# Banded attention with a top-1 expert layer on one core: the zero fill in two halves, the second round's up weights ahead of the row store

## The chip, the core and the metric

The program runs on one NeuronCore of a Trainium2 chip: a tensor engine (PE) with its own weight loads (PEld), VectorE (DVE), ScalarE (ACT), GpSimd (POOL), SyncE (SP), and 16 DMA engines that the queues of SP, ACT and POOL share. The metric is device microseconds for one execution.

## The reference

Two stages. The first is attention over 2 batches, 8 heads, 768 positions and 64 channels, in which each query sees the keys less than 16 positions away and one summary key and value for every block of 32 positions. The second is an expert layer over the 1536 tokens that result:

```python
logits = x @ w_gate
expert_idx = np.argmax(logits, axis=1)
...
for i in range(N):
    e = expert_idx[i]
    if counts[e] < capacity:
        disp[e, counts[e]] = x[i]
        ...
h = np.maximum(np.einsum('ecd,edf->ecf', disp, w1), 0.0)
y = np.einsum('ecf,efd->ecd', h, w2)
out = np.zeros((N, D), dtype=np.float32)
for i in range(N):
    if keep[i]:
        out[i] = gate_w[i] * y[expert_idx[i], pos[i]]
```

There are 8 experts of 512 x 1024 and 1024 x 512 weights and a capacity of 384 tokens. A row of `out` that no expert writes stays zero.

## The kernel before, in words

**Order.** Every operation has a short name, and the list `SEQ` (line 112) names them one after the other. An engine runs its own instructions in the order in which that list issues them. The framework adds the semaphore waits that the data need, and for DRAM tensors these go by the range of rows that an access names.

**Attention (to about 75 us).** For each batch and pair of heads the scores, their maximum, the exponentials, the turned probabilities and the product with the values run in groups of four blocks of 64 queries. The result of a batch lies in SBUF as `X[b]`: six tiles of 128 tokens, 512 channels, the token's number and its gate weight.

**Routing (`Route`), once per batch.** PE turns `X[b]` and multiplies it by the gate matrix; DVE finds each token's expert and its place there. At its end (`ga0`, `ga1`, line 439) SP stores the batch's rows into the DRAM tensor `xrow`.

**Expert rounds (`Round`).** A round serves one expert with up to 384 tokens. The first (names without a letter) takes an expert's tokens of batch 0 while batch 1 is still being routed; the second (B) and the third (C) take tokens of both batches. Seven more rounds stand in branches that this data does not enter. In a round:

- `lw` and `lW`: SP loads four quarters of the up weights `w1` and four of the down weights `w2`, 512 KB each, into the buffers `w1r` (tag `ld`) and `w2r`.
- `h` and `s`: ACT rounds each quarter to a high part, DVE takes the low rest (lines 580 and 586).
- `fr`: POOL gathers 128 rows of `xrow` by the numbers in `ids` into `xgb` (line 571), three times.
- `T`, `H`, `I`: PE turns the rows (line 599), ACT and DVE split them.
- `u`, `r`, `e`: the up product in eight pieces (line 625), the ReLU on ACT (630), the rest on DVE (634).
- `D`: the down product in three pieces of 128 tokens (line 642); `y`: ACT scales it by the gate weight (652).
- `P`: POOL writes the 128 rows of `y` to `out` by their token numbers (line 655); padded places have numbers beyond the bound and are dropped.

**The zero fill.** `zr` sets one tile `zrow` to zero on POOL, and `fill` lets SP write it over all of `out` (line 731). A put must come behind the fill of the rows that its access names, since the put's rows have to survive.

**What else sets the order.** The second round's gather reads all of `xrow` and so needs the stores of both batches. The first round's gather names batch 0 alone. The choice of the third round's expert reaches SP by a register load of `r0ei` (line 661), ahead of which SP stands until DVE has written it.

Of the kernel before, what the change touches and what calls it, by code (L numbers as in the profile page):

```python
# [10 lines left out]
F32 = mybir.dt.float32  # L11
# [26 lines left out]
NTOK = N // P  # L38
TPB = S // P
# [5 lines left out]
EARLY = TPB  # L45
# [65 lines left out]

SEQ = """
q1 k1 t0 S0 k2 z2 t2 S1 M0 q2 Q11a M1 Q10p E0 w1p q3 kb1 E1 S2 kp1p vb0 R0 z3 R1 M2 t1 K0 S3 K1 k3 kb2 E2 v0 w2p vt0 M3 v2 vk0 vb2 S4 kp2p E3 vP0 v1
R2 Q21a M4 S5 q4 Q20p K2 t3 E4 Q30p k4 R3 M5 Q31a vp0 S6 vb1 E5 zr misc t4 R4 M6 w3p q6 S7 K3 kb3 v3 E6 vt1 M7 V00 kp3p q5 vk1 K4 V01 vp1 N00 N00 vP1
R5 N01 N01 E7 S8 K5 R6 M8 S9 K6 E8 R7 M9 vt2 vk2 V10 E9 vP2 V11 N10 N10 Q41a Q40p S10 N11 N11 K7 vp2 k5 vb3 R8 S11 M10 t5 K8 w4p kb4 E10 R9 M11 vt3
kp4p V20 vk3 K9 vP3 V21 N20 E11 vb4 S12 vp3 N21 t6 N20 Q60p k6 Q61a N21 R10 M12 k7 R11 K10 S13 E12 vt4 K11 M13 V30 vk4 V31 E13 Q50p N30 N30 S14 N31
Q51a N31 w5p kb5 R12 x0 M14 K12 kp5p x1 vb5 X0a x2 X1a S15 t7 vb6 X2a q7 E14 v6 vt5 M15 l00 w6p vk5 kb6 v5 R13 L00a E15 R14 w7p v4 kb7 x3 g00 K13 v7
S16 X3a kp6p vb7 K14 vP4 x4 M16 x5 Q70p X4a S17 X5a vp4 Q71a vt6 kp7p E16 M17 l01 vp5 R15 vP5 L01a E17 S18 vk6 g01 K15 M18 vp6 R16 ch0 S19 vP6 E18 ch0
ch0 ch0 ch0 R17 ch0 ch0 M19 S20 ch0 ga0 E19 ga0 ga0 pf0 ga0 pick vt7 M20 V40 vk7 pick pl0 K16 pl0 vP7 pick V41 N40 pl0 K17 N40 S21 N41 pick vp7 N41
pick pl0 pl0 pl0 R18 pick pl0 pl0 E20 R19 V50 pl0 pl0 pl0 pl0 K18 pick M21 V51 K19 N50 pick N50 E21 tk0 S22 N51 pick pick pick pick first N51 lw0 ts0  # L120
pads rows lw1 pads R20 rows pads M22 rows fr0 lw2 S23 K20 lw3 pads E22 pads pads pads firstB R21 fr1 M23 K21 V60 E23 V61 fr2 N60 N60 h10a R22 N61 N61
R23 K22 s10v V70 K23 h11a V71 lW0 lW1 lW2 lW3 fill N70 N70 T0 N71 s11v x6 H0 x7 N71 X6a I0 X7a h12a o0 x8 X8a l10 s12v h13a o1 s13v T1 L10a T2 H1 o2
x9 H2 I1 g10 X9a I2 h20a x10 u0 X10a s20v h21a h22a s21v x11 r0 s22v u1 X11a h23a e0 s23v l11 r1 e1 u2 L11a g11 r2 u3 ch1 e2 ch1 ch1 ch1 ch1 ch1 ch1
u4 r3 ch1 e3 ga1 ga1 ga1 ga1 pf1 r4 cl1 lwB0 u5 pl1 pl1 pl1 lwB1 pl1 e4 pl1 pl1 pl1 pl1 u6 r5 pl1 pl1 pl1 pl1 padsB e5 padsB padsB padsB padsB padsB
padsB tk1 r6 u7 ts1 rd e6 rd rowsB rd rowsB frB0 lwB2 rd rd rd rd rd r7 rd rd rd e7 D0 rd rd frB1 rd rd hB10a rd rd rd rd rd rd rd rd rd set firstC
frB2 lwB3 lWB0 lWB1 lWB2 sB10v lWB3 hB11a nr lwC0 sB11v y0 frC0 lwC1 TB0 hB12a D1 HB0 sB12v P0 lwC2 IB0 hB13a sB13v lwC3 TB1 y1 frC1 TB2 HB1 D2 HB2
IB1 IB2 P1 hB20a sB20v hB21a lWC0 sB21v hB22a lWC1 sB22v uB0 hB23a lWC2 sB23v TC0 rB0 lWC3 uB1 y2 eB0 oB0 frC2 uB2 rB1 P2 hC10a eB1 sC10v rB2 uB3 eB2
oB1 TC1 rB3 uB4 hC11a eB3 sC11v uB5 rB4 eB4 rB5 uB6 hC12a eB5 sC12v uB7 rB6 oB2 eB6 rB7 HC0 eB7 DB0 HC1 IC0 hC13a IC1 sC13v TC2 yB0 PB0 DB1 HC2 IC2
oC0 DB2 yB1 PB1 hC20a sC20v hC21a sC21v hC22a oC1 sC22v uC0 hC23a yB2 PB2 sC23v uC1 rC0 eC0 rC1 uC2 eC1 oC2 uC3 rC2 eC2 rC3 uC4 eC3 uC5 rC4 eC4 rC5
uC6 eC5 uC7 rC6 eC6 rC7 eC7 DC0 DC1 yC0 PC0 DC2 yC1 PC1 yC2 PC2  # L130
""".split()


# [1 line left out]
def attention_moe(ctx: ExitStack, tc: tile.TileContext, qT, kT, vT, vw, wg, w1, w2, cf, cm, cr, cv, out, cap: int):  # L135
    nc = tc.nc
# [5 lines left out]
    big = ctx.enter_context(tc.tile_pool(name="big", bufs=4))  # L142
    work = ctx.enter_context(tc.tile_pool(name="work", bufs=2))
# [22 lines left out]
    r7 = cft[:, C_R7 : C_R7 + E]  # L166
# [24 lines left out]
    kc, qc, vc, vt, kt = {}, {}, {}, {}, {}  # L191
# [313 lines left out]
    bufs = {}  # L505
# [13 lines left out]
    class Round:  # L519
# [131 lines left out]
            self.y[j] = work.tile([P, DM], F32, tag="y", name="y", bufs=2)  # L651
            nc.scalar.activation(self.y[j], self.yp[j], AF.Copy, scale=self.xg[:, j, DM + 1 : DM + 2])  # L652

        def put(self, j):
            nc.gpsimd.indirect_dma_start(  # L655
                out=out, out_offset=bass.IndirectOffsetOnAxis(ap=self.oid[j], axis=0),
                in_=self.y[j], in_offset=None, bounds_check=N - 1, oob_is_err=False,
            )

    def fetch(t, hi, engines=(SP,)):  # L660
# [38 lines left out]
    sel, plans, ops = {}, [], {}  # L699
# [3 lines left out]
    def op(name, f, *a):  # L703
        ops[name] = lambda: f(*a)

    def op_on(name, f, *a):
        for e, eng in ENGINES.items():
            op(name + e, f, *a, eng)

    def chain(name, make):  # L710
        going = []

        def run():
            if not going:
# [9 lines left out]
        nc.scalar.dma_start(out=crt, in_=cr)  # L724

    def zeros():
        sel["zrow"] = work.tile([P, DM], F32, tag="y", name="zrow", bufs=2)
        nc.gpsimd.memset(sel["zrow"], 0.0)

    def fill():  # L730
        nc.sync.dma_start(out=out.rearrange("(t p) d -> p t d", p=P), in_=sel["zrow"].unsqueeze(1).to_broadcast([P, NTOK, DM]))

    def pick():
        key = const.tile([P, E], F32, name="key0")
# [97 lines left out]
    def last_clip():  # L832
        sel["cl"] = clip(RB.cn, "b")

    for c in range(2 * HP):
        op(f"k{c}", load_k, c)
        op(f"q{c}", load_q, c)
        op(f"t{c}", load_vt, c)
        op(f"v{c}", load_v, c)
        op_on(f"w{c}", windows, c)  # L840
        for h in range(2):
            op_on(f"Q{c}{h}", queries, c, h)
            op(f"V{c}{h}", values, c, h)
# [13 lines left out]
    for r, rt in enumerate(routes):  # L857
# [8 lines left out]
        op(f"pf{r}", rt.prefix)  # L866
        chain(f"pl{r}", rt.place)
        chain(f"ga{r}", rt.gate)
    for name, f in dict(misc=misc, zr=zeros, fill=fill, nr=count, set=settle, tk0=census, tk1=last_census, ts0=first_tokens, ts1=all_tokens, cl1=last_clip).items():
        op(name, f)  # L870
    for name, f in dict(pick=pick, rd=lambda: rounds(0)).items():
        chain(name, f)
# [1 line left out]
    def on_round(i, name, f, *a):  # L874
        op(name, lambda: getattr(R[i], f)(*a))

    for i, c in enumerate(["", "B", "C"]):
        op(f"first{c}", begin, i)
        if i < 2:
            chain(f"rows{c}", lambda i=i: rows(i))  # L880
            chain(f"pads{c}", lambda i=i: pads(i))
        for g in range(4):
            on_round(i, f"lw{c}{g}", "load_w1", (g,))
            on_round(i, f"lW{c}{g}", "load_w2", (g,))
            for e, eng in ENGINES.items():
                on_round(i, f"h{c}1{g}{e}", "high_w1", g, eng)
                on_round(i, f"s{c}1{g}{e}", "low_w1", g, eng)
                on_round(i, f"h{c}2{g}{e}", "high_w2", g, eng)
                on_round(i, f"s{c}2{g}{e}", "low_w2", g, eng)
        for j in range(RT):  # L890
            op(f"fr{c}{j}", rows_fetch, i, j)
            on_round(i, f"T{c}{j}", "turn", j)
            on_round(i, f"H{c}{j}", "turn_high", j)
            on_round(i, f"I{c}{j}", "turn_low", j)
            on_round(i, f"D{c}{j}", "down", j)
            on_round(i, f"o{c}{j}", "place", j)
            on_round(i, f"y{c}{j}", "weigh", j)
# [62 lines left out]
```

## Time and profile before

| | us |
|---|---|
| median of 3 runs | 194.74 (193.93 to 194.79) |
| the profiled execution | 196.38 |
| its span | 194.4 |
| PE busy | 175.4 |
| PE weight loads busy | 155.8 |
| ACT busy | 105.0 |
| DVE busy | 102.5 |
| POOL busy | 58.2 |

The rows below come from the profiled execution, whose span lies between its first and its last instruction. The table gives the busy time of each engine in that span; as matmuls are pipelined, a busy PE is not one at its peak. The transfers move 38.77 MB, 33.43 of it through SP's queue.

### The profile page before, as it was taken

Reading aid. Unit: us, or ns where it says so; the run is one execution under the profiler, and the core shown is the slowest. Engines: PE = TensorE matmul, PEld = TensorE weight load, DVE = VectorE, ACT = ScalarE, POOL = GpSimd, SP = SyncE. Lnnn points to the kernel's source line nnn. Section 1 sums busy time; section 2 is a strip of 40 time slices with the busy share of each in tenths; the row PEclk is TensorE's granted clock in tenths of the full one; section 3 lists DMA queues with packets and bytes.
Section 4 is the critical chain, followed back from the end, with each engine's and each line's share of the span. In section 5 each row is a group of like instructions: output and inputs, shape, how many; then the busy total and the mean of one; then the engine's idle time right before and its main releaser. Section 6 shows DMA issues by size and latency. Waiting matters only on the chain.

```text
span 194.4 us, 3977 instructions
## 1 busy us (share of the span) xinstructions
PE 175.4 (90%) x1461; PEld 155.8 (80%) x1461; DVE 102.5 (53%) x227; ACT 105.0 (54%) x228; POOL 58.2 (30%) x80
## 2 busy tenths in 40 slices
PE   7598979999899967999996899999999999999950
PEld 2487869899689956899994788999888899988840
DVE  2585747797279558875785628465620742310000
ACT  5779778898957868962236347534521832211110
POOL 7599725669533420000015430400021020002210
PEclk9999999999999999999999999999999999999998
DMA  6999999939948599991899999930001110001011
GB/s 178 372 335 225 252 319 254 330 147 292 258 143 290 141 310 378 392 404 63 273 270 361 390 370 366 385 129 0 3 8 46 54 54 5 0 2 47 8 64 56
DMA packets 20215, 38.77 MB, mean 199 GB/s; under 512 B 1450, under 2 KB 8284, under 8 KB 20188
## 3 DMA queue, kind: packets, MB, share of 16 engines
q1 hardware_dynamic: 18256, 33.43, 53.9%
q0 software_dynamic: 1440, 4.73, 6.4%
q10 hardware_dynamic: 492, 0.28, 0.7%
q8 instruction: 13, 0.21, 0.5%
q14 instruction: 14, 0.11, 0.2%
HBM read 29.77 MB, written 8.66 MB: 198 GB/s over the span
## 4 chain that ended last, share of the span: by engine, by line
issue 28%; PE 27%; DMA 25%; ACT 7%; DVE 5%; POOL 4%; SPq 1%; POOLq 0%; ACTq 0%
DMA out<-y,oid 11%; PE hp L625 9%; DMA kc<-kT 5%; PE sc L285 5%; DMA xgb<-xrow,aids 4%; PE yp L642 4%; DMA xgb<-xrow,bids 3%; ACT prob L294 3%; DMA qc<-qT 2%; PE pt L299 2%; PE xp L346 2%; PE av L313 1%; PE lq L357 1%; PE xgp L599 1%; DVE x L324 1%
## 5 line engine op out<-in xcount | busy, mean ns | idle before, releaser
L642 PE MATMUL yp<-w,h 128*128 128x512 f32 x216 | 50.4, 391 | 0.0
L642 PEld LDWEIGHTS yp<-w,h 128*128 128x128 f32 x216 | 40.3, 188 | 8.2
L625 PE MATMUL hp<-xh,w1h 128*128 128x384 f32 x96 | 32.9, 342 | 0.0
L625 PE MATMUL hp<-xl,w1h 128*128 128x384 f32 x96 | 32.2, 336 | 0.0
L625 PE MATMUL hp<-xh,w1l 128*128 128x384 f32 x96 | 32.2, 336 | 0.0
L285 PE MATMUL sc<-k,qb 128*128 128x120 f32 x192 | 26.6, 281 | 4.0 <-POOL qb L222 1.3
L630 ACT ACTIVATE h<-hp 128x384 fp32r<-128x384 f32 x24 | 11.8, 492 | 32.6 <-PE hp L625 31.1
L294 ACT ACTIVATE prob<-sc,nm 128x120 f32<-128x120 f32 x96 | 26.8, 371 | 3.9 <-PE pt L299 2.5
L285 PEld LDWEIGHTS sc<-k,qb 128*128 128x128 f32 x192 | 23.3, 191 | 6.6 <-POOL qb L228 1.9
L655 POOL DMA_INDIRECT out<-y,oid x9 | 9.7, 1081 | 58.4 <-ACT y L652 57.5
L634 DVE SCALAR_TENSOR_TENSOR h<-hp,h 128x384 fp32r<-128x384 f32 x24 | 13.3, 555 | 18.9 <-ACT h L630 18.9
L290 DVE TENSOR_REDUCE nm<-sc 128x4 f32<-128x480 f32 x24 | 15.6, 651 | 12.2 <-PE sc L286 8.0
L652 ACT ACTIVATE y<-yp,xgb 128x512 f32<-128x512 f32 x9 | 6.2, 686 | 27.7 <-PE yp L642 18.2
L625 PEld LDWEIGHTS hp<-xh,w1h 128*128 128x128 f32 x96 | 18.0, 188 | 0.3 <-issue 0.2
L586 DVE TENSOR_TENSOR w<-w2r,w 128x1024 fp32r<-128x1024 f32 x12 | 14.6, 1224 | 6.7 <-ACT w L232 5.6
L625 PEld LDWEIGHTS hp<-xl,w1h 128*128 128x128 f32 x96 | 18.0, 188 | 0.1
L625 PEld LDWEIGHTS hp<-xh,w1l 128*128 128x128 f32 x96 | 18.0, 188 | 0.0
L580 DVE TENSOR_TENSOR w1l<-w1r,w1h 128x1024 fp32r<-128x1024 f32 x12 | 14.7, 1222 | 4.6 <-ACT w1h L232 3.9
L228 POOL TENSOR_SCALAR v<-vrow 25x1040 f32<-25x1040 f32 (+1 forms) x16 | 13.4, 840 | 9.9 <-ACT vrow L268 9.0
L303 ACT COPY pts<-pt 121x512 f32<-121x512 f32 x24 | 13.8, 594 | 4.7 <-PE pt L299 3.9
L313 PE MATMUL av<-v,pts 121*64 121x65 f32 x384 | 13.8, 224 | 2.4 <-DMA v<-vw 1.2
L313 PEld LDWEIGHTS av<-v,pts 121*64 121x64 f32 x384 | 12.4, 137 | 4.1 <-issue 3.0
(124 smaller groups left out, 222.9 us busy)
## 6 DMA issues: line engine op xcount, KB each, us to landing
w1r<-w SPq DMA_DIRECT2D x12, 512.0 KB
w2r<-w SPq DMA_DIRECT2D x12, 512.0 KB
v<-vw SPq DMA_DIRECT2D x16, 292.5 KB
kc<-kT SPq DMA_DIRECT2D x8, 400.0 KB
xrow<-x SPq DMA_DIRECT2D x2, 1542.0 KB
vc<-vT SPq DMA_DIRECT2D x8, 384.0 KB
out<-zrow SPq DMA_DIRECT2D x1, 3072.0 KB
qc<-qT SPq DMA_DIRECT2D x7, 384.0 KB
```

Of the source, the lines that this page charges most:

```text
L228: eng.tensor_scalar(out=dst, in0=src, scalar1=f, scalar2=0.0, op0=ALU.mult, op1=ALU.add)
L285: nc.tensor.matmul(self.sc[:, i, :], qb[c % NQ][:, t, :], kt[c][:, t, :], start=i == 0, stop=False)
L290: nc.vector.tensor_reduce(out=self.nm, in_=self.sc, op=ALU.max, axis=AX.X, negate=True)
L294: nc.scalar.activation(self.pr[:, i, :KW], self.sc[:, i], AF.Exp, bias=self.nm[:, i : i + 1])
L303: nc.scalar.copy(self.pts[:KV], self.pt[:KV])
L313: nc.tensor.matmul(av[c, h][o : o + QT, ip, hh, :], G[3 * c + t // 4].pts[:KV, P * i + QT * hh : P * i + QT * hh + QT], vt[c][:KV, t, hh, ...
L580: eng.tensor_tensor(out=self.w1l[g], in0=self.w1r[g], in1=self.w1h[g].bitcast(F32), op=ALU.subtract)
L586: eng.tensor_tensor(out=self.w2[g][:, 1], in0=self.w2r[g], in1=self.w2[g][:, 0].bitcast(F32), op=ALU.subtract)
L625: nc.tensor.matmul(ps, a[g][:, kk, fo : fo + P], x[:, kk, :], start=n == 0, stop=n == 3 * KD - 1)
L630: nc.scalar.activation(self.h[f // 2][:, f % 2, 0], self.hp[f], AF.Relu)
L634: nc.vector.scalar_tensor_tensor(out=h[:, f % 2, 1], in0=self.hp[f], scalar=0.0, in1=h[:, f % 2, 0].bitcast(F32), op0=ALU.max, op1=ALU.sub ...
L642: nc.tensor.matmul(ps, self.h[g][:, i, a, P * j : P * j + P], self.w2[g][:, w, i, :], start=n == 0, stop=n == 3 * KF - 1)
```

## The change

The fill is cut by batch. `fill0` stands where `fill` stood and writes the rows of batch 0; `fill1` stands behind the last load of the third round and writes those of batch 1. The puts of the first round name only the rows of batch 0, so that they need `fill0` alone. The four loads of the second round's up weights, which stood behind the store of batch 1 (three of them ahead of the register load, one behind it), now follow the first round's last split of its up weights. `zr` goes from the early attention part to the end of the attention part, and its tile to another pool tag.

```diff
@@ SEQ (excerpts) @@
-R2 Q21a M4 S5 q4 Q20p K2 t3 E4 Q30p k4 R3 M5 Q31a vp0 S6 vb1 E5 zr misc t4 ...
+R2 Q21a M4 S5 q4 Q20p K2 t3 E4 Q30p k4 R3 M5 Q31a vp0 S6 vb1 E5 misc t4 ...
...
-R23 K22 s10v V70 K23 h11a V71 lW0 lW1 lW2 lW3 fill N70 N70 T0 N71 ... h13a o1 s13v T1 L10a
+R23 K22 s10v V70 K23 h11a V71 lW0 lW1 lW2 lW3 fill0 N70 N70 T0 N71 ... h13a o1 s13v lwB0 lwB1 lwB2 lwB3 T1 L10a
...
     def put(self, j, upto=N):
         nc.gpsimd.indirect_dma_start(
-            out=out, out_offset=bass.IndirectOffsetOnAxis(ap=self.oid[j], axis=0),
-            in_=self.y[j], in_offset=None, bounds_check=N - 1, oob_is_err=False,
+            out=out[:upto], out_offset=bass.IndirectOffsetOnAxis(ap=self.oid[j], axis=0),
+            in_=self.y[j], in_offset=None, bounds_check=upto - 1, oob_is_err=False,
         )
...
     def zeros():
-        sel["zrow"] = work.tile([P, DM], F32, tag="y", name="zrow", bufs=2)
+        sel["zrow"] = big.tile([P, DM], F32, tag="vc", name="zrow", bufs=2)
         nc.gpsimd.memset(sel["zrow"], 0.0)

-    def fill():
-        nc.sync.dma_start(out=out.rearrange("(t p) d -> p t d", p=P), in_=sel["zrow"].unsqueeze(1).to_broadcast([P, NTOK, DM]))
+    def fill(b):
+        rows = out[S * b : S * (b + 1)].rearrange("(t p) d -> p t d", p=P)
+        nc.sync.dma_start(out=rows, in_=sel["zrow"].unsqueeze(1).to_broadcast([P, TPB, DM]))
...
-            on_round(i, f"P{c}{j}", "put", j)
+            on_round(i, f"P{c}{j}", "put", j, P * EARLY if i == 0 else N)
```

On SP, from the fill to the register load, the program before has this (`w1r` are the second round's up weights, `x_99` is batch 1, an ISA row sets up a register):

```order
L731 DMA out<-zrow 128x12x512
L439 DMA xrow<-x_99 128x6x514
L562 ISA
L562 DMA w1r_1082<-w 128x4x256
L562 ISA
L562 DMA w1r_1091<-w 128x4x256
L562 ISA
L562 DMA w1r_1109<-w 128x4x256
L661 TENSOR_LOAD r0ei
L661 ISA x2
L562 ISA
L562 DMA w1r_1119<-w 128x4x256
```

The store is SP's next transfer behind the whole fill, and the loads follow it. The same stretch of SP in the changed program:

```order
L732 DMA out<-zrow 128x6x512
L562 ISA
L562 DMA w1r_1082<-w 128x4x256
L562 ISA
L562 DMA w1r_1091<-w 128x4x256
L562 ISA
L562 DMA w1r_1109<-w 128x4x256
L562 ISA
L562 DMA w1r_1119<-w 128x4x256
L439 DMA xrow<-x_99 128x6x514
L661 TENSOR_LOAD r0ei
L661 ISA x2
```

All four loads now stand ahead of the store, and the register load follows it directly.

On SP, at the end of the third round's loads (`w2r` are its down weights), the changed program has one more transfer ahead of the branch:

```order
L567 ISA
L567 DMA w2r_1237<-w 128x2x512
L567 ISA
L567 DMA w2r_1239<-w 128x2x512
L732 DMA out<-zrow 128x6x512
L918 COMPARE_AND_BRANCH
```

Before, the branch (L915 there) followed the last `w2r` at once. On POOL, the last gather of the third round and the puts around it, the two programs against each other:

```order
 L571 DMA xgb<-xrow,r0ids 128x514
-L655 DMA out<-y,oid 1536x512 x7
-L915 COMPARE_AND_BRANCH
+L655 DMA out<-y,oid 768x512
+L655 DMA out<-y,oid 1536x512 x6
+L918 COMPARE_AND_BRANCH
```

The order is the same; the first round's third put, like its other two, names 768 rows instead of 1536.

## Rows read from the trace of the kernel before

**Rows 1.** The page, busy tenths of PE and of the DMA engines in 40 slices.

```profile
PE   7598979999899967999996899999999999999950
...
DMA  6999999939948599991899999930001110001011
```

**Rows 2.** PE's waits from 80 us to the end: us in total, times, longest.

```profile
PE xgp L599 <- DMA xgb<-xrow,bids: 2.3, 1, 2.3
```

**Rows 3.** Timeline of PE around 105 us: start, us, instruction, idle before.

```profile
99.69 5.64 PE L642 MATMUL yp<-w,h 128*128 128x512 f32 x24
107.61 0.66 PE L599 MATMUL xgp<-cft,xgb 128*128 128x128 f32 x4 [2.28 <-DMA xgb<-xrow,bids]
...
114.38 5.70 PE L642 MATMUL yp<-w,h 128*128 128x512 f32 x24
```

**Rows 4.** Timeline of DVE.

```profile
77.61 1.23 DVE L580 TENSOR_TENSOR w1l<-w1r,w1h 128x1024 fp32r<-128x1024 f32 x1
...
98.67 0.18 DVE L492 TENSOR_REDUCE bids<-bpk 128x3 int32<-128x24 f32 x1
...
109.88 1.23 DVE L580 TENSOR_TENSOR w1l<-w1r,w1h 128x1024 fp32r<-128x1024 f32 x1 [0.26 <-ACT w1h L232]
```

**Rows 5.** Timeline of POOL.

```profile
18.71 0.53 POOL L728 MEMSET zrow<- 128x512 f32 x1
...
65.56 1.22 POOL L571 DMA_INDIRECT xgb<-xrow,aids  x1 [5.70 <-DVE apad L501]
...
101.15 1.00 POOL L571 DMA_INDIRECT xgb<-xrow,bids  x1 [31.75 <-DVE nai L806]
...
123.56 1.03 POOL L571 DMA_INDIRECT xgb<-xrow,r0ids  x1 [6.46 <-ACT y L652]
...
144.16 1.00 POOL L655 DMA_INDIRECT out<-y,oid  x1 [18.25 <-ACT y L652]
```

**Rows 6.** Timeline of SP's queue, issues merged; the fourth row is the last of the third's four.

```profile
72.11 0.65 SPq L731 DMA_DIRECT2D out<-zrow  x1
92.43 0.37 SPq L439 DMA_DIRECT2D xrow<-x  x1
93.04 8.35 SPq L562 DMA_DIRECT2D w1r<-w  x4
...
101.01 0.38 SPq L562 DMA_DIRECT2D w1r<-w  x1
...
101.69 2.98 SPq L567 DMA_DIRECT2D w2r<-w  x4
...
118.42 4.46 SPq L567 DMA_DIRECT2D w2r<-w  x4
```

**Rows 7.** Line L571, the nine gathers.

```profile
DMA to landing us min/median/max: 5.9/6.4/8.0
```

**Rows 8.** Line L655, the puts from 107 to 117 us, then from 143 us on.

```profile
DMA to landing us min/median/max: 6.0/6.3/6.6
...
DMA to landing us min/median/max: 2.7/2.7/4.3
```

**Rows 9.** Windows: us, busy of PE, PEld, DVE, ACT, POOL, PEclk, DMA share, GB/s.

```profile
65.00:70.00 5.00, 4.00 (x63) 3.46 (x63) 0.97 (x4) 4.09 (x11) 3.23 (x3) 1.00 0.81 223
82.00:87.00 5.00, 5.00 (x50) 4.52 (x50) 4.36 (x5) 3.57 (x6) 0.00 (x0) 1.00 1.05 408
89.00:91.00 2.00, 2.00 (x14) 2.00 (x13) 1.35 (x7) 0.22 (x1) 0.00 (x0) 1.00 0.02 9
93.40:97.00 3.60, 3.60 (x22) 3.60 (x21) 3.38 (x15) 0.49 (x1) 0.00 (x0) 1.00 1.06 358
97.00:98.00 1.00, 1.00 (x17) 0.84 (x17) 0.31 (x3) 0.49 (x1) 0.00 (x0) 1.00 0.99 144
102.00:104.00 2.00, 2.00 (x10) 1.68 (x9) 1.51 (x4) 1.53 (x2) 1.39 (x3) 1.00 1.09 347
128.00:130.00 2.00, 2.00 (x15) 1.96 (x14) 0.55 (x1) 1.07 (x2) 0.00 (x0) 1.00 0.11 41
```

More of the change, by code (lines that the diff above doesn't have):

```diff
@@ L113 @@
 q1 k1 t0 S0 k2 z2 t2 S1 M0 q2 Q11a M1 Q10p E0 w1p q3 kb1 E1 S2 kp1p vb0 R0 z3 R1 M2 t1 K0 S3 K1 k3 kb2 E2 v0 w2p vt0 M3 v2 vk0 vb2 S4 kp2p E3 vP0 v1
-R2 Q21a M4 S5 q4 Q20p K2 t3 E4 Q30p k4 R3 M5 Q31a vp0 S6 vb1 E5 zr misc t4 R4 M6 w3p q6 S7 K3 kb3 v3 E6 vt1 M7 V00 kp3p q5 vk1 K4 V01 vp1 N00 N00 vP1
-R5 N01 N01 E7 S8 K5 R6 M8 S9 K6 E8 R7 M9 vt2 vk2 V10 E9 vP2 V11 N10 N10 Q41a Q40p S10 N11 N11 K7 vp2 k5 vb3 R8 S11 M10 t5 K8 w4p kb4 E10 R9 M11 vt3
-kp4p V20 vk3 K9 vP3 V21 N20 E11 vb4 S12 vp3 N21 t6 N20 Q60p k6 Q61a N21 R10 M12 k7 R11 K10 S13 E12 vt4 K11 M13 V30 vk4 V31 E13 Q50p N30 N30 S14 N31
@@ L117 @@
-Q51a N31 w5p kb5 R12 x0 M14 K12 kp5p x1 vb5 X0a x2 X1a S15 t7 vb6 X2a q7 E14 v6 vt5 M15 l00 w6p vk5 kb6 v5 R13 L00a E15 R14 w7p v4 kb7 x3 g00 K13 v7
-S16 X3a kp6p vb7 K14 vP4 x4 M16 x5 Q70p X4a S17 X5a vp4 Q71a vt6 kp7p E16 M17 l01 vp5 R15 vP5 L01a E17 S18 vk6 g01 K15 M18 vp6 R16 ch0 S19 vP6 E18 ch0
-ch0 ch0 ch0 R17 ch0 ch0 M19 S20 ch0 ga0 E19 ga0 ga0 pf0 ga0 pick vt7 M20 V40 vk7 pick pl0 K16 pl0 vP7 pick V41 N40 pl0 K17 N40 S21 N41 pick vp7 N41
+R2 Q21a M4 S5 q4 Q20p K2 t3 E4 Q30p k4 R3 M5 Q31a vp0 S6 vb1 E5 misc t4 R4 M6 w3p q6 S7 K3 kb3 v3 E6 vt1 M7 V00 kp3p q5 vk1 K4 V01 vp1 N00 N00 vP1 R5
@@ new lines @@
+N01 N01 E7 S8 K5 R6 M8 S9 K6 E8 R7 M9 vt2 vk2 V10 E9 vP2 V11 N10 N10 Q41a Q40p S10 N11 N11 K7 vp2 k5 vb3 R8 S11 M10 t5 K8 w4p kb4 E10 R9 M11 vt3 kp4p
+V20 vk3 K9 vP3 V21 N20 E11 vb4 S12 vp3 N21 t6 N20 Q60p k6 Q61a N21 R10 M12 k7 R11 K10 S13 E12 vt4 K11 M13 V30 vk4 V31 E13 Q50p N30 N30 S14 N31 Q51a
+N31 w5p kb5 R12 x0 M14 K12 kp5p x1 vb5 X0a x2 X1a S15 t7 vb6 X2a q7 E14 v6 vt5 M15 l00 w6p vk5 kb6 v5 R13 L00a E15 R14 w7p v4 kb7 x3 g00 K13 v7 S16
+X3a kp6p vb7 K14 vP4 x4 M16 x5 Q70p X4a S17 X5a vp4 Q71a vt6 kp7p E16 M17 l01 vp5 R15 vP5 L01a E17 S18 vk6 g01 K15 M18 vp6 R16 ch0 S19 vP6 E18 ch0 ch0
@@ L120 @@
+ch0 ch0 R17 ch0 ch0 M19 S20 ch0 ga0 E19 ga0 ga0 pf0 ga0 pick vt7 M20 V40 vk7 pick pl0 K16 pl0 vP7 pick V41 N40 pl0 K17 N40 S21 N41 pick vp7 zr N41
 pick pl0 pl0 pl0 R18 pick pl0 pl0 E20 R19 V50 pl0 pl0 pl0 pl0 K18 pick M21 V51 K19 N50 pick N50 E21 tk0 S22 N51 pick pick pick pick first N51 lw0 ts0
 pads rows lw1 pads R20 rows pads M22 rows fr0 lw2 S23 K20 lw3 pads E22 pads pads pads firstB R21 fr1 M23 K21 V60 E23 V61 fr2 N60 N60 h10a R22 N61 N61
-R23 K22 s10v V70 K23 h11a V71 lW0 lW1 lW2 lW3 fill N70 N70 T0 N71 s11v x6 H0 x7 N71 X6a I0 X7a h12a o0 x8 X8a l10 s12v h13a o1 s13v T1 L10a T2 H1 o2
@@ L123 @@
[L123 to L130, printed above, removed]
+R23 K22 s10v V70 K23 h11a V71 lW0 lW1 lW2 lW3 fill0 N70 N70 T0 N71 s11v x6 H0 x7 N71 X6a I0 X7a h12a o0 x8 X8a l10 s12v h13a o1 s13v lwB0 lwB1 lwB2
@@ new lines @@
+lwB3 T1 L10a T2 H1 o2 x9 H2 I1 g10 X9a I2 h20a x10 u0 X10a s20v h21a h22a s21v x11 r0 s22v u1 X11a h23a e0 s23v l11 r1 e1 u2 L11a g11 r2 u3 ch1 e2 ch1
+ch1 ch1 ch1 ch1 ch1 u4 r3 ch1 e3 ga1 ga1 ga1 ga1 pf1 r4 cl1 u5 pl1 pl1 pl1 pl1 e4 pl1 pl1 pl1 pl1 u6 r5 pl1 pl1 pl1 pl1 padsB e5 padsB padsB padsB
+padsB padsB padsB tk1 r6 u7 ts1 rd e6 rd rowsB rd rowsB frB0 rd rd rd rd rd r7 rd rd rd e7 D0 rd rd frB1 rd rd hB10a rd rd rd rd rd rd rd rd rd set
+firstC frB2 lWB0 lWB1 lWB2 sB10v lWB3 hB11a nr lwC0 sB11v y0 frC0 lwC1 TB0 hB12a D1 HB0 sB12v P0 lwC2 IB0 hB13a sB13v lwC3 TB1 y1 frC1 TB2 HB1 D2 HB2
@@ new lines @@
+IB1 IB2 P1 hB20a sB20v hB21a lWC0 sB21v hB22a lWC1 sB22v uB0 hB23a lWC2 sB23v TC0 rB0 lWC3 fill1 uB1 y2 eB0 oB0 frC2 uB2 rB1 P2 hC10a eB1 sC10v rB2
+uB3 eB2 oB1 TC1 rB3 uB4 hC11a eB3 sC11v uB5 rB4 eB4 rB5 uB6 hC12a eB5 sC12v uB7 rB6 oB2 eB6 rB7 HC0 eB7 DB0 HC1 IC0 hC13a IC1 sC13v TC2 yB0 PB0 DB1
+HC2 IC2 oC0 DB2 yB1 PB1 hC20a sC20v hC21a sC21v hC22a oC1 sC22v uC0 hC23a yB2 PB2 sC23v uC1 rC0 eC0 rC1 uC2 eC1 oC2 uC3 rC2 eC2 rC3 uC4 eC3 uC5 rC4
+eC4 rC5 uC6 eC5 uC7 rC6 eC6 rC7 eC7 DC0 DC1 yC0 PC0 DC2 yC1 PC1 yC2 PC2
@@ L652, in weigh, with put @@
             nc.scalar.activation(self.y[j], self.yp[j], AF.Copy, scale=self.xg[:, j, DM + 1 : DM + 2])
-        def put(self, j):
+        def put(self, j, upto=N):
             nc.gpsimd.indirect_dma_start(
-                out=out, out_offset=bass.IndirectOffsetOnAxis(ap=self.oid[j], axis=0),
-                in_=self.y[j], in_offset=None, bounds_check=N - 1, oob_is_err=False,
+                out=out[:upto], out_offset=bass.IndirectOffsetOnAxis(ap=self.oid[j], axis=0),
+                in_=self.y[j], in_offset=None, bounds_check=upto - 1, oob_is_err=False,
             )
@@ L833, in last_clip @@
         sel["cl"] = clip(RB.cn, "b")
+    for b in range(B):
+        op(f"fill{b}", fill, b)
     for c in range(2 * HP):
@@ L868, in attention_moe @@
         chain(f"ga{r}", rt.gate)
-    for name, f in dict(misc=misc, zr=zeros, fill=fill, nr=count, set=settle, tk0=census, tk1=last_census, ts0=first_tokens, ts1=all_tokens, cl1=last_clip).items():
+    for name, f in dict(misc=misc, zr=zeros, nr=count, set=settle, tk0=census, tk1=last_census, ts0=first_tokens, ts1=all_tokens, cl1=last_clip).items():
         op(name, f)
```

## The prediction

> **What bounds the kernel now.** I began with the slices of the page [rows 1]. Each slice is 4.86 us. From the one at 78 us on PE's row shows nines until the last two slices, but for a 6 at 102 us and the 8 behind it. The DMA row shows four slices at 9 before a 1 at 87 us: the transfers run dry for a moment and start again. So the bound is PE's order of work, and a change can win only where PE stands idle.
>
> The waits of PE from 80 us to the end are one single row: 2.3 us for `xgb<-xrow,bids`, the rows of the second round [rows 2]. PE's timeline shows the place: the first third of round one's down product ends at 99.69 + 5.64 = 105.33 us, and the transposes of the gathered rows start at 107.61, after 2.28 us of idleness [rows 3]. The last scaling, the last put and the end of the span hang on PE's last product, so what is won here stays won unless another wait takes its place.
>
> Next, what makes those rows late. DVE has the row numbers `bids` ready at 98.67 + 0.18 = 98.85 [rows 4]. POOL starts the gather at 101.15, 2.30 us later [rows 5]. The profile names DVE's `nai` at L806 as the releaser, but `nai` is no input of the gather; what it needs besides `bids` is the store of the second batch's rows into `xrow`, which SP issued at 92.43 [rows 6]. Part of the 2.30 us must be POOL's own way from a release to a start, so the store holds the gather up by less than that.
>
> Then the gather itself. From issue to landing the nine gathers of the trace take 5.9 to 8.0 us, 6.4 in the middle [rows 7]. POOL's puts are the same kind of transfer, 128 rows of about 2 KB: while SP's loads are running they take 6.0 to 6.6 us, and from 143 us on, where the DMA row shows 0 to 1, the median is 2.7 [rows 1, 8]. So some 3.7 us of a gather is waiting beside SP's loads. At 101.15 these are round two's up weights: their issues begin at 93.04, right behind the store, and the fourth goes out at 101.01, after a register load that waits for DVE [rows 6].
>
> **The change part by part.**
>
> *Up weights of round two ahead of the store.* Four loads of 512 KB move from behind the `xrow` store to right behind the fill, which SP issues at 72.11 [rows 6]. Each needs a buffer that DVE's split of round one has read; the last of the four splits ends at 77.61 + 1.23 = 78.84 [rows 4], so SP can issue all four by about 80, and the store, which waits for DVE until 92.4, is not kept from its issue.
>
> What the queue has to carry before the store: now 3072 KB of fill, 3.15 MB at 408 GB/s = 7.7 us, dry at about 89.0 (share 0.02 behind it) [rows 9]; so the fill began at 81.3. Then half of it, 3.86 us, until 85.2, and 2.10 MB of up weights at 347 GB/s, the rate of such loads from 102 to 104 us [rows 9], 6.0 us, until 91.2. The store runs at full share from 93.4 on [rows 9], so 2.2 us are left. Bound: at 223 GB/s, the rate while round one's up weights began [rows 9], they take 9.4 us, until 94.6, and push the store back by 1.2 us.
>
> What stood behind the store is gone: no load follows it until the register load is through at about 101. Its rate falls from 358 to 144 GB/s now, when the first up weights come in [rows 9]. I take 0.45 us for that, of the 2.30 us above at most, and nothing at least: the gather starts at 100.7.
>
> *The gather in the shorter queue.* Ahead of it is at most the first of round two's down weights, which now takes the issue slot at 101.01; the others follow 0.7 us apart (four in 2.98) [rows 6]. The lower end is the empty queue, 2.7 us, the upper end the slowest gather, 8.0 [rows 7, 8]. I take 2.7 plus one load of 512 KB at 347 GB/s, 1.5 us, together 4.2: the queue is nearly empty at that moment, so the puts' row is the nearer one. Landing at 100.7 + 4.2 = 104.9, before PE is free at 105.33. PE's 2.28 us go completely, with 0.4 us to spare.
>
> A rule of the Trainium skill speaks against this ("DMA: Bandwidth & Descriptors", section "Queues, rings and completion order"): each DMA engine takes turns between the queues that have work, a packet at a time. By it the depth of SP's queue would matter little to a gather, which comes through another queue, and the sum would hold the store's 0.45 us alone, 194.3 us in all, against 192.5 by the rows. The puts at 6.0 to 6.6 against 2.7 us [rows 8] do not agree with so small an effect of a busy queue.
>
> *What is late next.* Behind the transposes PE waits for nothing [rows 2], so the question is what becomes late when everything moves 2.28 us forward. Round two's up weights are split at 109.88 + 1.23 = 111.1 [rows 4] and now sooner, since the loads are; PE needs them at 114.38 + 5.70 - 2.28 = 117.8 [rows 3]. The splits of its down weights write buffers that PE's own products must first have read, and move along. The gain stays 2.28; if this cover failed, the first product of round two would wait for DVE instead.
>
> *Second half of the fill behind round three's loads.* SP issues the last of these at 118.42 + 4.46 = 122.88 [rows 6], 120.6 in the new time. Its 1536 KB take 3.9 us at 408 GB/s, behind loads that are through by 128 (share 0.11 from there) [rows 9], 125.7 in the new time: 129.6, and with a quiet put's 2.7 us at most, 132.3. Two things wait on it. Round two's first put has one more wait; it starts at 144.16 now [rows 5], 141.9 then, with only the other puts behind it on POOL. Cover 9.6 us. The third round's last gather, started at 123.56 [rows 5], 121.3 then, may come 3.9 us later, at 121.3 + 8.0 + 3.9 = 133.2 at the latest; its rows are wanted beside that same put, near 141. Cost 0; without that cover, up to 3.9 us.
>
> *Puts bounded to batch 0.* Three puts keep their time on POOL (1.00 us for the one at 144.16 [rows 5]); the bound lets them wait for the first half of the fill alone, long landed. Cost 0, between -0.3 and 0.3.
>
> *The memset moved.* 0.53 us of POOL go at 18.71 and come again right ahead of the first gather, where POOL stands idle for 5.70 us [rows 5]. Cost 0. The place at 18.71 lies in the attention part, on no row that I read; I allow a gain of 0.3 and no loss.
>
> **Sum.** -2.28 us and nothing against it. The profiled execution took 196.38 us, 194.4 of it span; it becomes 194.1. The median of the runs is 194.74, 1.64 below that execution, and becomes 194.74 - 2.28 = 192.46, say 192.5.
>
> **The rivals.**
>
> *The gather is no faster.* No gather of the trace was seen in an empty queue, and a gather reads rows where a put writes them; what takes 6.4 us may be the gather and not the queue [rows 7]. Then it lands at 100.7 + 6.4 = 107.1 and 0.45 us are won: 194.3, no change. Against it stand the puts [rows 8]. Chance 0.14; the rule on turns between queues says the same.
>
> *The moved loads delay the store (the other side).* At 223 GB/s the queue is dry at 94.6, the store is 1.2 us later and the gather starts at 101.15 + 1.2 - 0.45 = 101.9. If it then takes the 8.0 us of the slowest one, because the down weights crowd in at that moment, it lands at 109.9 where PE has the rows at 107.6 now [rows 3], 2.3 us later: 197.0, slower. It decides from a landing behind 107.6 on, and passes 0.5% behind 108.6. For it: round one's up weights did run at that rate beside gathers [rows 9]. Against it: the slices at 9 from 68 to 87 us [rows 1], where the moved loads go. Chance 0.08.
>
> *Only part of the wait goes.* The store late by 1.2 us, the gather at 4.2: landing at 106.1, 0.8 us of waiting left, 193.3. I count it with the forecast; its own range is 191.8 to 193.6.
>
> **How the numbers follow.** Forecast 0.78 (with the part case), no faster gather 0.14, delayed store 0.08. The runs before spread from 193.93 to 194.79, 0.86 us, so 0.5%, about 1 us, is the smallest difference that I take for one. Faster, below 193.8: 0.76, since a little of the part case falls short. Same 0.16, slower 0.08. The range runs from 191.7 (the forecast less 0.3 for the memset and 0.4, half the spread) to 194.5, which takes in the gather that is no faster.
>
> **What would show it.** Right: no idle time of PE before the transposes at L599, which start near 105.4 us; the gather of `bids` starting between 99.8 and 101.2 and landing in 3 to 4.7 us; the store issued at 92.4 as before; the second fill issued near 120.6 and no wait of POOL on it at 142. Wrong: a gather that still takes 6 us although no up weights are in flight, a store that is issued or lands later than now, or a new gap of PE behind 105 us.

## The result and the profile after

| | before | changed |
|---|---|---|
| median of 21 runs, us | 195.79 (193.93 to 198.26) | 193.30 (191.17 to 194.29) |
| the profiled execution, us | 196.38 | 193.34 |
| its span, us | 194.4 | 191.4 |
| PE idle before round two's transposes, us | 2.28 | 0 |
| gather of round two: start to landing, us | 6.4 | 3.4 |

The ratio of the changed kernel to the one before is 0.9885, 95% interval 0.9861 to 0.9908: 1.15% of 195.8 is 2.25 us, with an interval from 1.80 to 2.72. The ratio leaves out the runs that lie more than 1.5% above the fastest of the same kernel; the medians of all runs are 2.49 us apart. The forecast was 2.28 us and 192.5. With 21 runs the median of the kernel before came out 1.05 us above that of the first three.

PE and the DMA engines of the changed kernel, in 40 slices of its page [rows 1 are those of before]:

```profile
PE   7778899999999976999999999999999999999950
...
DMA  6999999939969499997627999991010110001011
```

PE's 6 at 102 us is gone: from the slice at 77 us on there are nines up to the last two slices. In the DMA row the slice at 87 us now holds a 7 where a 1 stood, the moved loads, and the slice at 96 us has become a 2: the pause now lies behind the store. The 9 at 124 us, where a 3 stood, is the late half of the fill.

PE's waits from 78 us on, in the changed kernel (us in total, times, longest) [rows 2]:

```profile
PE xp L346 <- DVE xl L607: 0.3, 1, 0.3
```

The row for `xgb<-xrow,bids` is gone and none has come in its place. PE's timeline at the same spot [rows 3]:

```profile
99.09 5.65 PE L642 MATMUL yp<-w,h 128*128 128x512 f32 x24
104.58 0.60 PE L599 MATMUL xgp<-cft,xgb 128*128 128x128 f32 x4
104.93 5.75 PE L642 MATMUL yp<-w,h 128*128 128x512 f32 x24
```

The transposes follow the product without an idle time. POOL's timeline [rows 5] and the landing of its gather at 98.8 [rows 7]:

```profile
98.83 1.00 POOL L571 DMA_INDIRECT xgb<-xrow,bids  x1 [29.78 <-DVE r0ki L466]
...
141.13 0.99 POOL L655 DMA_INDIRECT out<-y,oid  x1 [17.39 <-ACT y L652]
```

```profile
L571 POOL DMA_INDIRECT xgb<-xrow,bids x1: 997/997/997, 98.8 to 98.8; - x1
...
DMA to landing us min/median/max: 3.4/3.4/3.4
```

The rows are there at 102.2, 2.4 us before PE wants them. SP's issues [rows 6]:

```profile
71.65 0.53 SPq L732 DMA_DIRECT2D out<-zrow  x1
72.42 10.72 SPq L562 DMA_DIRECT2D w1r<-w  x4
91.82 0.37 SPq L439 DMA_DIRECT2D xrow<-x  x1
100.65 2.75 SPq L567 DMA_DIRECT2D w2r<-w  x4
...
119.88 0.56 SPq L732 DMA_DIRECT2D out<-zrow  x1
```

From the store's issue to the gather's start it was 101.15 - 92.43 = 8.72 us before and is 98.83 - 91.82 = 7.01 now. DVE's row numbers [rows 4]:

```profile
98.07 0.18 DVE L492 TENSOR_REDUCE bids<-bpk 128x3 int32<-128x24 f32 x1
```

They are ready at 98.25, and the gather starts 0.58 us later; before, it started 2.30 us behind them. In each of the thirteen profiles they are ready 6.42 or 6.43 us behind the store's issue. So the store now holds the gather up by 0.58 us at most, and part of that must be POOL's own way to a start: a still earlier store would win next to nothing. The windows of the changed kernel (PE, PEld, DVE, ACT, POOL, PEclk, DMA share, GB/s) [rows 9]:

```profile
89.00:91.00 2.00, 2.00 (x13) 2.00 (x12) 1.09 (x6) 0.62 (x2) 0.00 (x0) 1.00 0.34 109
91.00:92.50 1.50, 1.50 (x18) 1.34 (x17) 0.75 (x5) 0.24 (x1) 0.00 (x0) 1.00 0.00 0
93.40:97.00 3.60, 3.60 (x33) 3.44 (x32) 2.77 (x12) 0.71 (x2) 0.00 (x0) 1.00 1.02 359
97.00:98.00 1.00, 1.00 (x8) 1.00 (x7) 0.92 (x6) 0.27 (x1) 0.00 (x0) 1.00 0.10 35
98.00:100.00 2.00, 2.00 (x12) 1.84 (x11) 1.79 (x12) 0.71 (x2) 1.00 (x1) 1.00 0.00 0
...
130.00:132.00 2.00, 2.00 (x13) 2.00 (x12) 0.58 (x2) 1.43 (x2) 0.00 (x0) 1.00 0.04 11
```

The queue is dry before the store, the store is nearly through by 97 (share 0.10 in the microsecond behind it), and nothing moves from 98 to 100. The late half of the fill is over before 132, and the put at 141.13 waits for ACT, not for it.

### The profile page after: what moved, and what is told of

It is laid out like the page before. It is cut to its first block, busy times and chain, and to the rows that moved or that the text cites. A ratio compares the mean times of both kernels' runs of the same rounds, so it can differ in the third digit from the quotient of the medians.

```text
span 191.4 us, 3979 instructions
## 1 busy us (share of the span) xinstructions
PE 175.1 (92%) x1461; PEld 156.1 (82%) x1461; DVE 102.4 (53%) x227; ACT 104.5 (55%) x228; POOL 59.2 (31%) x80
## 5 line engine op out<-in xcount | busy, mean ns | idle before, releaser
L285 PE MATMUL sc<-k,qb 128*128 128x120 f32 x192 | 27.3, 286 | 3.7 <-POOL qb L222 1.3
L655 POOL DMA_INDIRECT out<-y,oid x9 | 10.7, 1185 | 61.1 <-ACT y L652 56.7
L285 PEld LDWEIGHTS sc<-k,qb 128*128 128x128 f32 x192 | 24.0, 196 | 6.3 <-POOL qb L228 1.8
L232 ACT CAST w<-w2r 128x1024 fp32r<-128x1024 f32 x12 | 12.6, 1060 | 3.1 <-PE yp L642 2.5
L299 PE MATMUL pt<-cft,prob 128*121 128x128 f32 x96 | 14.1, 278 | 0.0
```

The costliest lines, as they stand in the source:

```text
L285: nc.tensor.matmul(self.sc[:, i, :], qb[c % NQ][:, t, :], kt[c][:, t, :], start=i == 0, stop=False)
L299: nc.tensor.transpose(self.pt[:KV, P * i : P * i + P], self.pr[:, i], ident)
L655: nc.gpsimd.indirect_dma_start(out=out[:upto], out_offset=bass.IndirectOffsetOnAxis(ap=self.oid[j], axis=0), in_=self.y[j], in_offset=None ...
```

## The experiments

Each ratio is to the kernel before, on the same chip, with its 95% interval; all were timed in five rounds but for the one with the unbounded puts, which had three. PE's granted clock, the share of its full clock that it was given, differs from run to run; where runs are sorted by it below, the line is a mean of 0.985 over the run. The 21 runs of the changed kernel have none between 0.980 and 0.988.

### The loads early, the fill whole

```diff
 SEQ of before
-... h13a o1 s13v T1 L10a ...   (lwB0 to lwB3 at their four later places)
+... h13a o1 s13v lwB0 lwB1 lwB2 lwB3 T1 L10a ...
```

> Kernel before, with one edit: the four up-weight loads of round two moved ahead of the batch-1 store; the zero fill stays whole and in its place. My theory (what counts is what stands in SP's queue behind the store): the queue now carries 3.1 MB of fill and 2.1 MB of weights before the store and is dry near 94.6 us instead of 90.7, so the store lands about 1.3 us later than in the changed kernel (99.4), the gather starts near 100.2 and takes 3.4 to 4.5 us; PE waits 0 to 0.5 us for it; 1.8 to 2.3 us faster than before, ratio 0.988 to 0.991. Rival (the halved fill is what wins, the loads only use the room): the store is held up behind the full queue, PE waits 1.5 us or more, ratio 0.996 or above.

Measured: 0.9951 (0.9913 to 0.9990), some 1 us and not 2. My expectation failed by half; the rival had the mechanism, a store held up and a wait of 1.5 us or more. PE still waits, and the gather takes 5.7 us (PE's waits, then line L571 at 99.2, then the windows before the store):

```profile
PE xgp L599 <- DMA xgb<-xrow,bids: 1.9, 1, 1.9
```

```profile
DMA to landing us min/median/max: 5.7/5.7/5.7
```

```profile
91.00:92.50 1.50, 1.50 (x11) 1.50 (x10) 1.50 (x9) 0.05 (x1) 0.00 (x0) 1.00 1.05 362
92.50:94.00 1.50, 1.50 (x10) 1.50 (x9) 1.50 (x6) 0.49 (x1) 0.00 (x0) 1.00 1.04 380
```

and its SP and POOL:

```profile
90.13 0.37 SPq L439 DMA_DIRECT2D xrow<-x  x1
98.72 2.23 SPq L567 DMA_DIRECT2D w2r<-w  x4
```

```profile
99.17 1.00 POOL L571 DMA_INDIRECT xgb<-xrow,bids  x1 [31.97 <-DVE r0eq L479]
```

The queue is full when the store is issued at 90.13, so the gather starts 9.04 us later, 2.62 us behind its row numbers. By then the register load has let the down weights go, at 98.72, 0.45 us ahead of the gather; in the changed kernel the gather starts 1.82 us ahead of them. A late store costs twice: the gather starts later, and starts behind loads. A wait of 1.9 us is only 0.4 less than in the one profile of before, so it does not account for the whole 1 us; where the rest comes from is not shown.

### The fill split, the loads late

```diff
 SEQ of after
-... s13v lwB0 lwB1 lwB2 lwB3 T1 ...
+... s13v T1 ...   (lwB0 to lwB3 back at their places of before)
```

> The changed kernel with one part undone: the four up-weight loads stand where they stood before, behind the store; the split fill, the bounded puts and the moved memset stay. My theory: the fill alone buys nothing, the queue was dry before the store anyway; gather near 101 us, 6 us or more to landing, PE waits 2.0 to 2.5 us; ratio 0.997 to 1.003. Rival (less write traffic before the store is the gain): ratio near 0.99.

Measured: 0.9955 (0.9913 to 0.9997), just below the range that I gave and less than half of the change. It is not clear of nothing: sorted by granted clock, its runs took 194.6 us on average at 0.985 or above (seven) and 195.9 below (five), those of the kernel before beside it 194.5 (twelve) and 196.1 (seventeen). The gather starts at 99.57 and takes 6.0 us, since the up weights are issued from 91.96 on, right behind the store; PE waits 1.4 us, less than in the one profile of before. This trace has the store's landing:

```profile
DMA to landing us min/median/max: 7.5/7.5/7.5
```

The two halves of the change give 0.49% and 0.45% by themselves and 1.15% together. These intervals are too wide to tell the whole from the sum of its parts; that the fill makes the room that the loads take is read from the full queue in the profile of the loads early with the whole fill.

### The loads later than before

```diff
 SEQ of before
-... set firstC frB2 ...   (lwB0 to lwB3 earlier)
+... set firstC lwB0 lwB1 lwB2 lwB3 frB2 ...
```

> Kernel before, with one edit: the four up-weight loads go the other way, behind the register load of r0ei, so that SP issues them from about 100.7 us, after the store has landed; fill whole. My theory: the store has the engines to itself and lands in 6.2 us, the gather starts near 98.9 and is ahead of most of the loads, landing in 3.4 to 4.7 us, by 103.6; PE does not wait for it; the split up weights are ready by about 113, before PE needs them at 117.8; ratio 0.988 to 0.991, without touching the fill. Rival (early weights are what wins, since splits and casts start sooner): no gain or a new wait of PE for DVE near 117 us, ratio 0.997 or above.

Measured: 0.9963 (0.9922 to 1.0004). The gather did what was expected, the time did not:

```profile
L571 POOL DMA_INDIRECT xgb<-xrow,bids x1: 1000/1000/1000, 99.6 to 99.6; - x1
...
DMA to landing us min/median/max: 3.4/3.4/3.4
```

The store, with nothing behind it, lands sooner than the 7.5 us of the run above:

```profile
DMA to landing us min/median/max: 6.3/6.3/6.3
```

Nothing waits for `bids` any more, but PE's and ACT's waits have new rows:

```profile
PE xgp L599 <- DVE xl L607: 1.6, 1, 1.6
```

```profile
ACT w1h L232 <- DMA w1r<-w: 7.5, 1, 7.5
```

ACT stands 7.5 us for the second quarter of the up weights, and the casts of the gathered rows stand behind it in ACT's and DVE's order. So a gather with the queue to itself takes 3.4 us whether the loads come earlier or later, and the loads cannot come as late as this because their splits then stand in the way of the rows. Here the rival was right about the time, within the interval, and the theory about the gather; the new wait of PE ends at 113.4 us, for DVE's split of the gathered rows, and is not one near 117 for the weights.

### The fill behind the store

```diff
 SEQ of before
-... lW3 fill N70 ...   (lwB0 to lwB3 late)
+... lW3 N70 ... s13v lwB0 lwB1 lwB2 lwB3 T1 ... ga1 fill pf1 ...   (fill behind the fourth ga1)
```

> Kernel before, with the up-weight loads early and the whole 3 MB fill moved to directly behind the batch-1 store, so that other bytes stand where the weights stood. My theory (it is the queue, whatever it carries): the store is slowed as before, the gather starts near 100.5 and waits behind the fill, 6 us or more to landing; PE waits 1.5 to 2.5 us; ratio 0.996 to 1.003. Rival (engines take turns between the queues, depth does not matter; or it was the weight loads as such): gather 3 to 4 us, no wait of PE, ratio near 0.9885.

Measured: 1.0128 (1.0081 to 1.0174), slower. The gather starts at 98.90, which is 7.68 us behind the store's issue at 91.22: 0.67 us more than in the changed kernel, 1.04 less than before. The fill behind it slowed the store a little (it lands after 6.9 us, against 6.3 with nothing behind it). The gather then takes 8.3 us behind 3 MB of zeros, and PE waits:

```profile
L571 POOL DMA_INDIRECT xgb<-xrow,bids x1: 1000/1000/1000, 98.9 to 98.9; - x1
...
DMA to landing us min/median/max: 8.3/8.3/8.3
```

```profile
107.14 1.02 POOL L655 DMA_INDIRECT out<-y,oid  x1 [1.02 <-DMA out<-zrow]
```

```profile
104.00:107.20 3.20, 0.12 (x1) 0.00 (x0) 1.23 (x1) 1.62 (x2) 1.06 (x2) 1.00 1.00 309
107.20:111.00 3.80, 3.80 (x12) 3.12 (x13) 1.92 (x2) 1.53 (x2) 0.95 (x1) 0.56 1.04 393
111.00:113.00 2.00, 2.00 (x10) 1.58 (x10) 0.00 (x0) 0.00 (x0) 0.00 (x0) 0.97 1.05 402
```

The first put of round one needs the whole fill and is released at 107.14; the gathered rows land at 98.90 + 8.3 = 107.2, together with the end of the fill. So it is not the weight loads as such: other bytes in their place hold the gather up too, and more of them hold it up for longer (6.4 us before, 3.4 in an empty queue). POOL itself spends 1.00 us on the gather in each of these profiles, so the difference arises behind its issue; how, no run shows. The Trainium skill states that each DMA engine takes turns between the queues ("DMA: Bandwidth & Descriptors", section "Queues, rings and completion order"). My rival took from this that depth does not matter and that the gather takes 3 to 4 us; the 8.3 us do not agree with it. Behind the wait of 3.1 us PE's clock fell: 0.56 granted on average over 3.8 us. At full clock the same work would take some 2.1 us (an estimate, 0.56 x 3.8), so this run loses more than the wait is longer.

### The puts unbounded

```diff
-            on_round(i, f"P{c}{j}", "put", j, P * EARLY if i == 0 else N)
+            on_round(i, f"P{c}{j}", "put", j)
```

> The changed kernel with one part undone: the first round's puts name all 1536 rows of out again, so that they wait for the second half of the fill too, which SP issues near 120 us and which lands near 131. My theory (the bound is what makes the late half free): the first put, due on POOL at 107, stands until about 131, the last two gathers of the third round stand behind it, and PE waits near 125 to 138 us; 8 to 13 us slower than the changed kernel, ratio to before 1.03 to 1.06. Rival (the bound does nothing): ratio 0.9885 as the changed kernel.

Measured: 0.9885 (0.9815 to 0.9956) from four runs, the changed kernel's ratio. I had the direction of the wait wrong. The first two puts stand ahead of the second fill in program order, so it is the fill that waits for them (2.5 us on SP, issue at 122.30 and not 119.88), and only the third put waits for the fill:

```profile
130.52 1.02 POOL L655 DMA_INDIRECT out<-y,oid  x1 [9.12 <-SPq L918]
140.97 1.00 POOL L655 DMA_INDIRECT out<-y,oid  x1 [9.44 <-ACT y L652]
```

It goes out 10 us before the next put is due, and no gather stands behind it. The bound takes 9 us of waiting off POOL that nobody waits for.

### The memset alone

```diff
 SEQ of before
-... E5 zr misc ... vp7 N41 ...
+... E5 misc ... vp7 zr N41 ...   (and the tile in tag "vc")
```

> Kernel before with one edit: the memset of the zero tile at its new place and in its new pool tag, nothing else. My theory: nothing waits for it at either place; ratio 0.996 to 1.004, PE's wait for the rows of round two stays near 1.5 to 2.3 us. Rival (the 0.6 us by which the changed kernel's profile was ahead at 99 us come from POOL's freed 0.53 us): ratio 0.997, and PE at its first down product near 99.1 us.

Measured: 1.001 (0.996 to 1.006). Its PE waits 1.6 us for `bids`, with SP's order as before: 2.28 and 1.6 are two single readings of the same wait. No effect, as forecast; the head start of single profiles at 99 us (97.17 here, 99.69 in that of before) is scatter of the attention part.

### A register load between, and matmuls in the wait

The changed kernel's profile has one wait of PE of 1.9 us, for the first round's gather near 70 us. It comes and goes with the execution: the profile of before has 0.3 us there, those of the loads early, the loads later and the fill behind the store 2.1 to 2.2, and those of the unbounded puts and the memset alone none. Two edits aim at it, apart and together:

```diff
 SEQ of after
-... lw0 ts0 pads ... pads firstB R21 ...
+... lw0 firstB ts0 pads ... pads R21 ...
```

```diff
+    def idle_matmuls():
+        ps = psum.tile([P, 4 * P], F32, name="idle", tag="pt")
+        for _ in range(7):
+            nc.tensor.matmul(ps, identb, cmt[:, : 4 * P], start=True, stop=True)
 ... N70 N70 T0 ...  ->  ... N70 N70 dm T0 ...
```

> The changed kernel with one edit: SP's second register load of the expert numbers moves from behind round one's four up-weight loads to behind the first of them, so that loads two to four are issued some 0.7 us later. If a gather lands behind the loads that were issued before it (as the runs so far say), the first round's gather has about two loads ahead instead of three, lands in 5 to 6 us instead of 7, and PE's wait for it falls from 1.9 us to 0.5 to 1.2; 0.4 to 1.2 us faster than the changed kernel, ratio to before 0.982 to 0.987. Rival (the up-weight splits end last there, and they become later): the same as the changed kernel or slower, ratio 0.988 to 0.994.

Measured: 0.9893 (0.9830 to 0.9956), not told apart from the changed kernel. That profile shows no wait for the gather, but 1.3 us of PE's time before it went to waits that the profile calls issue. The unbounded puts and the memset alone, timed beside it without this edit, show the same, so it settles nothing.

> The changed kernel with seven extra 128x512 bf16 matmuls on PE (some 1.5 us, their result read by nobody) right ahead of the first round's transposes, where PE waits about 1.9 us for the gathered rows. In part of the runs of every kernel the mean granted clock is 0.97 to 0.98 instead of 0.99, and one profile shows 0.50 from 73 to 78 us, behind that wait. If PE's idle time there brings the fall, the fall goes: nearly all runs at 0.985 or above, mean 0.5 to 0.8 us less than the changed kernel, ratio to before 0.984 to 0.987. Rival (the fall comes by itself): the same mix of clocks, ratio 0.9885 or some tenths of a microsecond worse.

Measured: 0.9932 (0.9895 to 0.9969). The clock did what was expected: all 12 runs at a mean granted clock of 0.985 or above, against 10 of 21 of the changed kernel (and 8 of 10 of the two variants without matmuls that were timed beside it). The time did not: seven matmuls end after the rows are there and cost more than the clock gives back.

> The changed kernel with three instead of seven extra 128x512 bf16 matmuls ahead of the first round's transposes (0.7 us, read by nobody). If a shorter idle time is enough to hold the clock: nearly all runs at 0.985 or above, and as the matmuls mostly lie in PE's wait, 0.3 to 0.6 us less than the changed kernel in the mean, ratio to before 0.984 to 0.988. Rival (the clock still falls in part of the runs, and the matmuls cost their time): ratio 0.989 to 0.993.

Measured: 0.9851 (0.9815 to 0.9887); 9 of 12 runs at 0.985 or above. The profiled one is among the low ones, and its clock fell at 10 us, far from these matmuls (last section). A thirteenth took 973.02 us at full clock; it is left out of both figures, and what held it up is not known.

> The changed kernel with both edits: the second register load between the first and the second up-weight load of round one, and the three extra matmuls. If the earlier gather and the held clock add up: 0.5 to 1.2 us less than the changed kernel, ratio to before 0.981 to 0.986. Rival (the up-weight splits end last there): as the changed kernel, 0.988 to 0.991.

Measured: 0.9841 (0.9799 to 0.9882), median 191.16 us, all 6 runs at 0.985 or above. Its PE loses 0.2 us to that gather, which lands in 6.0 us, where the changed kernel beside it has 7.1 and a wait of 2.0 (PE's waits, the edited kernel first):

```profile
PE xgp L599 <- DMA xgb<-xrow,aids: 0.2, 1, 0.2
```

```profile
PE xgp L599 <- DMA xgb<-xrow,aids: 2.0, 1, 2.0
```

In these runs the version is faster than both kernels: 191.16 us (190.96 to 192.29, six runs), against 193.37 (191.81 to 194.88, twelve) for the changed kernel run again, below. It is the best of four variants tried, on six runs, so its lead may be somewhat flattered; which of its two edits gives how much is not settled. Part of it is the clock: at 0.985 or above alone it is 191.3 us (six) against 192.1 (five) for the changed kernel and 192.0 (nine) with the three matmuls only.

> The changed kernel as it is, beside the two below and the kernel before on one chip. My theory: 0.9885 again, within 0.985 to 0.992; no wait of PE for the rows of round two; the store lands in 6 to 6.6 us from its issue; part of the runs at a mean clock below 0.985. Rival (its gain was luck of the first session): 0.993 or above, or a wait of PE of 1 us or more.

Measured: 0.9927 (0.9883 to 0.9970), median 193.37 us. The interval overlaps that of the first session, but its middle lies just outside the 0.985 to 0.992 that I gave. Sorted by granted clock the gain is there again: 192.1 us (five) against 194.1 (nine) of the kernel before at 0.985 or above, 194.0 (seven) against 196.5 (thirteen) below. The profile repeats: no wait for round two's rows, the gather in 3.3 us, 97.37 - 90.38 = 6.99 us from the store's issue to the gather's start.

## Why the prediction came out

- **The place.** Right: PE's only wait behind 80 us was the one for round two's rows, and the time fell by its 2.28 us within the interval. That nothing else is late behind it held as well: from round two's first transposes to the end of the span it is 194.4 - 107.61 = 86.8 us before and 191.4 - 104.58 = 86.8 now. That 2.25 comes so close to 2.28 is luck: the interval is some 0.45 us to either side, and the wait itself was 1.6 us in the profile of the memset alone. The time forecast, 192.5, was 0.8 below the median, as the three runs it started from were 1.05 low.
- **The store.** The mechanism held, the size did not: I took 0.45 us, the profile shows 8.72 - 7.01 = 1.71. The gather starts 0.58 us behind its row numbers instead of 2.30, so 1.7 of the 2.30 us, which the prediction had as its bound, was the store. I had charged the store only for the visible drop of its rate; its landing is 6.3 us from the issue with nothing behind it and 7.5 with the up weights behind it. The start at 98.83 lies outside the 99.8 to 101.2 that I gave, also when the 0.6 us by which this execution is ahead of that of before are added.
- **The gather.** 3.4 us against 4.2: it started early enough to be ahead of the down weights, not behind the first of them. With both gains taken too small the rows land at 102.2, not 104.9; as PE wants them at 104.6, the gain is the same. The forecast had 0.4 us to spare, the kernel has 2.4.
- **The room in the queue.** Right, with more to spare: 91.2 forecast, dry between 89 and 91 (share 0.34, then 0.00). SP could not issue all four loads by 80, though; the last went out at 83.1, still 8.7 us ahead of the store. That the halved fill is needed for it stood in the sum only as a bound on the store; the run with the whole fill puts the room at about half of the gain, with a wide interval.
- **The gather that is no faster (rival).** Refuted by the changed kernel, by the run with late loads (3.4 us in an empty queue) and by the run with the fill behind the store (8.3).
- **The delayed store (rival).** It did not come in the changed kernel. It did with the fill whole, and took about half of the gain.
- **The late fill, the memset.** Cost 0, as forecast: no wait at 141.13, and 1.001 for the memset alone.
- **The bounded puts.** Cost 0 as forecast, but my reason was incomplete: the puts ahead of the second fill would hold the fill up, not be held up by it.

## What to carry to other kernels

In these runs a small gather waited behind the bytes that were queued when it was issued, though they came through another queue: 3.4 us behind nothing, 6.4 behind weight loads, 8.3 behind 3 MB of zeros. Loads that go out during its issue count as well: the changed kernel's second gather started 0.52 us ahead of the first down weight and took 5.1 us. So look at what stands ahead of a small urgent transfer, and at how long before the next bulk load it starts. Bulk that can wait (zeros, late weights) belongs behind it, bulk that engines wait for ahead of what it depends on; each move needs room in the queue at its new place. Here the gain was the one wait that the change takes away, and that could be read from PE's waits beforehand, as far as a single profile tells it.

## What the runs showed of the hardware

PE's clock falls after its waits in some executions and not in others. One profile, of the kernel with the late loads, has PE waiting 2.1 us for the first gather, and behind it (windows as above):

```profile
68.00:73.00 5.00, 2.94 (x54) 2.46 (x49) 3.66 (x7) 2.59 (x5) 0.09 (x1) 0.96 1.05 374
73.00:78.00 5.00, 4.32 (x37) 3.36 (x37) 3.08 (x6) 4.20 (x7) 0.00 (x0) 0.50 1.06 386
78.00:82.00 4.00, 4.00 (x27) 4.00 (x26) 2.58 (x3) 3.41 (x6) 0.00 (x0) 0.82 1.04 398
```

0.50 is the lower of the two levels, 1.2 of 2.4 GHz. The changed kernel's first profile has a wait of 1.9 us at the same place and full clock behind it. Two more profiles show a fall, and neither lies behind that wait. The first is that of the three matmuls, where PE stands in the attention part, the second that of the unbounded puts, where 1.3 of 2 us go to waits that the profile calls issue:

```profile
9.00:10.00 1.00, 0.02 (x1) 0.00 (x0) 0.94 (x2) 0.97 (x5) 0.88 (x3) 1.00 0.96 339
11.00:12.00 1.00, 1.00 (x7) 1.00 (x6) 0.44 (x1) 0.20 (x1) 1.00 (x3) 0.50 0.98 373
```

```profile
66.00:68.00 2.00, 0.70 (x7) 0.41 (x6) 0.00 (x0) 1.09 (x2) 1.10 (x2) 1.00 0.91 272
71.00:72.00 1.00, 1.00 (x17) 0.88 (x14) 0.49 (x3) 0.00 (x0) 0.00 (x0) 0.50 1.05 382
```

Of the 21 runs of the changed kernel 11 had a mean clock under 0.985, and they took 193.6 us on average against 192.4 for the other ten; of 29 runs of the kernel before beside the first four experiments it was 17, 196.1 against 194.5. With matmuls in the wait the low runs became fewer (none of 12, 3 of 12, none of 6), but the two variants timed beside the seven matmuls had only 1 of 4 and 1 of 6 without any. Each fall in these profiles follows a stretch in which PE stood idle, near 70 us in some executions and elsewhere in others. That the matmuls in that one wait keep the clock up is likely but not shown, and what decides in a single execution stays open.
